# One row of the last weight's second part in four transfers of 25, 25, 64 and 14 partitions

## The chip, the cores and the metric

The kernel runs on one core of a Trainium2 chip. The metric is the device time of one execution in microseconds (us). Engines are named as the profile names them: PE (TensorE's matmuls), PEld (its weight loads), DVE (VectorE), ACT (ScalarE), POOL (GpSimd) and SP (SyncE); a q behind a name means its queue of instructions. Sixteen DMA engines serve the core and move all data between HBM and the on-chip memory.

## The reference

One token passes a transformer block. It is attention over a long cache, and then a gated feed-forward network; the batch is 1 and the query length is 1.

```python
h  = x + attention(layernorm(x), k_cache, v_cache, wq, wo)
# x [1,1,1024]; k_cache, v_cache [1,4,65536,128]; wq [1024,4096]; wo [4096,1024]
# attention: 32 heads of 128, 8 heads to each of 4 cache groups, softmax(q k / sqrt(128)) v
h2 = h + (gelu(layernorm(h) @ w_gate) * (layernorm(h) @ w_up)) @ w_down
# w_gate, w_up [1024,3584]; w_down [3584,1024]; all bfloat16
```

## The kernel before, in words

All weights and both caches are read from HBM once, in all 173 MB, into one buffer `ring` of four slots (`slot`, L183), 32 KB per partition each. All these transfers are issued on SP's queue, in the order of the code. Operations are recorded by `Flow.op` and `Flow.dma` (L31, L69) and issued by `Flow.issue` (L76) with the waits that follow from the keys they read and write, so most instructions carry line 95 in the profile.

The stages are: the layer norm and the query projection (wq, two transfers); eight attention steps, each with two transfers of K and one of V; the output projection (wo); the second layer norm; gate (w_gate, 7 MB), up (w_up, 7 MB) and down (w_down, 7 MB). Within the steps PE runs a loop (`pe_loop`, L415) that takes tokens from the other engines.

The change is in the down projection. Its 3,584 rows are laid on 128 partitions in two blocks. `wa` (L577) holds FA = 16 rows per partition, in slot 0, and is one transfer. `wb` (L578) holds the other FB = 12 rows per partition, in slot 1, and comes in three transfers (L582): FB - FZ = 8 rows, FZ - 1 = 3 rows and 1 row per partition. A row is 1,024 bfloat16 numbers, 2 KB. So a transfer of the eight rows moves 16 KB into each partition. In HBM a partition's twelve rows are one run of 24 KB (`wb_src`, L579).

Each of the four transfers has a landing semaphore: `r_sem[0]`, `r_sem[1]`, `k_sem[0]` and `k_sem[1]`. A transfer raises its semaphore by 16 in all when it has landed. `Flow.dma` gives back the count that the semaphore then has, and `parts` keeps it with the rows (L585).

`wa` is issued when gate's last matmul has read slot 0 (key R0). The others are behind it on SP's queue; their slot 1 (key R1) is free by then as well, and no other wait is between them.

After all recorded work PE runs the down projection (L600 to L605): for each part, four matmuls that keep it busy ahead of the first two parts (`stay_busy`, L596), a wait for the part's semaphore, and then eight matmuls of one row each (`down`, L590), 128 x 32 by 128 x 128, for each of the part's rows. In all these are 28 x 8 = 224 matmuls. They add into two banks that already hold h. Two casts, on DVE (L607) and ACT (L608), then write the result `h2`, and SP stores it (L609).

Of the kernel before, what the change touches and what calls it, by code (L numbers as in the profile page):

```python
# [108 lines left out]
def kernel(  # L109
# [14 lines left out]
    P = 128  # L124
# [58 lines left out]
    def slot(i, n=1):  # L183
        return ring[:, i * CW:(i + n) * CW]

    f = Flow(nc, tc)
# [312 lines left out]
    FA = CW // D  # L499
# [78 lines left out]
    wb = slot(1)[:, 0:FB * D].rearrange("p (e n) -> p e n", e=FB)  # L578
    wb_src = B_w_down[P * FA:F, :].rearrange("(p e) n -> p e n", p=P)  # L579
    parts = [(wa, 0, FA, f.dma("sp", wa, B_w_down[0:P * FA, :].rearrange("(p e) n -> p e n", p=P), after=["R0"], inc=(r_sem[0], 16)), r_sem[0])]  # L580
    e0 = 0
    for i, z in enumerate((FB - FZ, FZ - 1, 1)):  # L582
        part = wb[:, e0:e0 + z, :]
        s = (r_sem[1], k_sem[0], k_sem[1])[i]
        parts.append((part, FA + e0, z, f.dma("sp", part, wb_src[:, e0:e0 + z, :], after=["R1"] if i == 0 else [], inc=(s, 16)), s))  # L585
        e0 += z
    with tc.tile_critical(no_gpsimd_drain=True):
        f.issue()
# [51 lines left out]
```

## Time and profile before

| what | value |
|---|---|
| time, median of 3 runs | 409.96 us (409.71 to 410.44) |
| the profiled execution: its time, its span | 409.71 us, 407.8 us |
| busy: PE, PEld, DVE, ACT, POOL | 234.8, 105.8, 202.5, 39.5, 19.2 us |
| read from HBM | 173.02 MB, 424 GB/s over the span |
| w_down's four transfers issued by SP | from 377.01 us, 2.24 us in all |
| from issue to landing, w_down's 4096, 2048, 768 and 256 KB | 20.4, 25.0, 25.9 and 26.0 us |
| last weight load of the down projection | 404.85 us |
| the two casts | start at 405.34 us |
| the store of the result issued | 405.71 us |

The span reaches from the first to the last instruction of the program. The page divides it into 40 equal slices; a digit is the busy share of a slice in tenths, and the DMA row is the mean over the sixteen DMA engines. Beside instructions, the trace records each DMA packet (start, duration, bytes and queue, not the number of its engine) and each single increment of a landing semaphore. Times within the execution are from the start of the span.

### The profile page before, as it was taken

To read this page: it belongs to the slowest core of one execution; us is meant where nothing else is said; L and a number is where in the kernel's file an instruction comes from. 1 tells how busy PE (TensorE), PEld (TensorE's weight loads), DVE (VectorE), ACT (ScalarE), POOL (GpSimd) and SP (SyncE) were. 2 spreads that over 40 slices of the span, in tenths; PEclk is the share of its full clock that TensorE was granted. 3 is DMA by queue.
4 is the path that set the end of the run, shared out by engine and by line. 5 is a ranking of instruction groups with operands and counts; after the bars stand their busy time and mean duration, and the time that the engine had idled before them with its cause. 6 is when DMAs were issued, how large, how long until landed. Compare 5 with 4: busy or idle time off the path is not lost. (4 is left out here: it accounts for less than half of the span.)

```text
span 407.8 us, 3909 instructions
## 1 busy us (share of the span) xinstructions
PE 234.8 (58%) x1645; PEld 105.8 (26%) x1647; DVE 202.5 (50%) x174; ACT 39.5 (10%) x141; POOL 19.2 (5%) x39
## 2 busy tenths in 40 slices
PE   0433855585577368734973686557465747365376
PEld 0211322232232133212321232223132223142324
DVE  1218860876089328924781687089508941010210
ACT  1000003000300300030003000300220021000000
POOL 4210000001000000010000001000000000012000
PEclk9955995599569967978796689689976976565668
DMA  8999999999999999999998999999999999999995
GB/s 344 427 421 452 415 460 411 460 418 412 453 460 418 411 425 488 418 408 421 476 437 376 453 424 444 421 460 418 411 453 466 418 418 424 452 440 435 399 413 220
DMA packets 4815, 173.12 MB, mean 424 GB/s; under 512 B 580, under 2 KB 584, under 8 KB 840
## 3 DMA queue, kind: packets, MB, share of 16 engines
q1 hardware_dynamic: 4760, 173.02, 98.5%
q8 instruction: 5, 0.08, 0.1%
q14 instruction: 2, 0.02, 0.0%
q10 hardware_dynamic: 48, 0.00, 0.0%
HBM read 173.02 MB, written 0.00 MB: 424 GB/s over the span
## 5 line engine op out<-in xcount | busy, mean ns | idle before, releaser
L95 DVE STREAM_TRANSPOSE ktb<-ring 128x4096 f32<-128x4096 f32 x32 | 141.1, 4418 | 83.4 <-DMA ring<-in_A_k_cache_dram 83.4
L427 PE MATMUL bank<-ktb,qs 128*128 128x512 bf16 x512 | 132.6, 418 | 61.3 <-PEq L413 61.3
L427 PEld LDWEIGHTS bank<-ktb,qs 128*128 128x128 bf16 x512 | 51.5, 104 | 139.2 <-issue 93.6
L439 PE MATMUL bank<-ring,pt 128*32 128x512 bf16 x512 | 46.3, 541 | 36.5 <-PEq L413 36.5
L95 ACT ACTIVATE pt<-sc,nb 128x256 bf16<-128x256 f32 x64 | 31.5, 494 | 255.3 <-DVE nb L95 255.3
L439 PEld LDWEIGHTS bank<-ring,pt 128*32 128x32 bf16 x512 | 19.4, 131 | 60.2 <-issue 57.3
L95 DVE STREAM_TRANSPOSE sc<-bank 128x512 f32<-128x512 f32 x32 | 22.2, 695 | 24.6 <-PE bank L427 24.6
L95 PE MATMUL bank<-ring,xz 128*32 128x512 bf16 (+1 forms) x192 | 19.2, 587 | 17.2 <-DMA ring<-in_B_w_gate_dram 5.2
L95 DVE TENSOR_REDUCE mx<-sc 128x8 f32<-128x1536 f32 (+1 forms) x16 | 19.5, 1219 | 0.5
L95 DVE STREAM_TRANSPOSE ktb<-bank 128x512 f32<-128x512 f32 (+1 forms) x6 | 4.0, 672 | 31.3 <-PE bank L95 30.9
L95 POOL COPY qs<-qsel 32x128 bf16<-32x128 bf16 x16 | 7.8, 490 | 231.4 <-PE bank L427 216.8
L95 PEld LDWEIGHTS bank<-ring,xz 128*32 128x32 bf16 x192 | 7.5, 141 | 26.9 <-issue 15.9
L95 ACT ACTIVATION_READ_ACCUMULATOR pt<-sc,nb 128x1 f32 x64 | 12.0, 187 | 0.0
L448 PE MATMUL bank<-sel,acc_sb 128*128 128x8 f32 x64 | 8.2, 255 | 6.2 <-PEq L413 6.2
L431 PE MATMUL bank<-ident_f,mx 128*8 128x128 f32 x8 | 2.2, 269 | 14.6 <-PEq L413 14.6
L448 PEld LDWEIGHTS bank<-sel,acc_sb 128*128 128x128 f32 x64 | 7.7, 191 | 10.0 <-issue 10.0
L95 PE MATMUL bank<-ring,ktb 128*32 128x512 bf16 x64 | 6.4, 586 | 5.9 <-DMA ring<-in_A_wo_dram 5.9
L95 ACT COPY acc_sb<-bank 128x512 f32<-128x512 f32 x8 | 4.7, 586 | 48.9 <-PE bank L439 48.9
L95 DVE TENSOR_TENSOR h_col<-bank,x_col 128x8 f32<-128x8 f32 x1 | 0.2, 167 | 14.8 <-PE bank L95 14.8
L95 PE MATMUL bank<-sel,ktb 128*128 128x16 f32 (+1 forms) x24 | 5.2, 356 | 3.5 <-DVE bank L95 2.7
L95 POOL MEMSET ktb<- 128x1024 bf16 (+2 forms) x3 | 3.5, 1164 | 75.8 <-PE bank L427 75.8
L433 PE MATMUL bank<-diag,ones_f 8*128 8x8 f32 x16 | 3.7, 299 | 5.7 <-PEq L413 5.7
(85 smaller groups left out, 60.9 us busy)
## 6 DMA issues: line engine op xcount, KB each, us to landing
ring<-in_A_k_cache_dram SPq DMA_DIRECT2D x16, 4096.0 KB, 24.9
ring<-in_A_wq_dram SPq DMA_DIRECT2D x2, 4096.0 KB, 16.7
ring<-in_B_w_gate_dram SPq DMA_DIRECT2D x1, 7168.0 KB, 26.9
ring<-in_B_w_up_dram SPq DMA_DIRECT2D x1, 7168.0 KB, 27.2
ring<-in_B_w_down_dram SPq DMA_DIRECT2D x1, 4096.0 KB, 20.4
ring<-in_B_w_down_dram SPq DMA_DIRECT2D x1, 2048.0 KB, 25.0
ring<-in_B_w_down_dram SPq DMA_DIRECT2D x1, 768.0 KB, 25.9
ring<-in_B_w_down_dram SPq DMA_DIRECT2D x1, 256.0 KB, 26.0
```

Source lines behind the costliest of these rows:

```text
L95: ins = getattr(self.eng[e], o["call"])(**o["kw"])
L427: m = nc.tensor.matmul(bank[c][:], lhsT=qs[:, jt].rearrange("p s c -> p (s c)")[:, s * P:(s + 1) * P], rhs=mv[:, :, J, :, u], start=(s == ...
L431: nc.tensor.transpose(out=mxT_ps, in_=mx1[:], identity=ident_f[:]).then_inc(s_step, 1)
L433: nc.tensor.matmul(bc_ps, lhsT=ones_f[0:rep, :], rhs=diag[:], start=True, stop=True).then_inc(s_step, 1)
L439: m = nc.tensor.matmul(acc[32 * q:32 * q + 32, :], lhsT=pt[:, c, n, :, :].rearrange("p h s -> p (h s)"), rhs=v_sb[:, c, :, n, :], start=(c ...
L448: m = nc.tensor.matmul(o_ps, lhsT=acc_sb[:, u * Dh:(u + 1) * Dh], rhs=sel[:, u:SQ:NS], start=(u == 0), stop=(u == NS - 1))
```

## The change

The eight-row transfer of `wb` becomes five transfers. Row 0 of every partition goes first, in four: partitions 0 to 24, 25 to 49, 50 to 113 and 114 to 127. Rows 1 to 7 of all partitions follow in one. All five raise the same semaphore, `r_sem[1]`, by 16 each, and PE's wait for the part is for the count after the fifth. The three-row and the one-row transfer are as before, behind them on the queue. No matmul changes, nor the order of rows in which they run.

```diff
     for i, z in enumerate((FB - FZ, FZ - 1, 1)):
         part = wb[:, e0:e0 + z, :]
         s = (r_sem[1], k_sem[0], k_sem[1])[i]
-        parts.append((part, FA + e0, z, f.dma("sp", part, wb_src[:, e0:e0 + z, :], after=["R1"] if i == 0 else [], inc=(s, 16)), s))
+        if i == 0:
+            for p0, p1 in ((0, 25), (25, 50), (50, 114), (114, P)):
+                f.dma("sp", wb[p0:p1, 0, :], wb_src[p0:p1, 0, :], after=["R1"], inc=(s, 16))
+            at = f.dma("sp", part[:, 1:, :], wb_src[:, 1:z, :], after=["R1"], inc=(s, 16))
+        else:
+            at = f.dma("sp", part, wb_src[:, e0:e0 + z, :], inc=(s, 16))
+        parts.append((part, FA + e0, z, at, s))
         e0 += z
```

## The prediction

> **What bounds the kernel now.** I began with the profile's page: the DMA row by slice, the queues, then the chain that ended last.
>
> ```profile
> DMA  8999999999999999999998999999999999999995
> ...
> q1 hardware_dynamic: 4760, 173.02, 98.5%
> ...
> DVE h L607 0%
> ```
>
> The DMA engines are busy in every slice but the first and the last ones, and SP's queue alone fills 98.5% of sixteen engines' span. The chain stops at the last cast (L607), so what comes before that cast has to be read from the timeline of PE at the end and from PE's waits from 370 us on:
>
> ```profile
> 397.48 3.40 PE L593 MATMUL bank<-ring,ktb 128*32 128x128 bf16 x128
> 401.05 0.81 PE L598 MATMUL bank<-qs 128*128 128x512 bf16 x3 [0.16 <-issue]
> 402.38 0.62 PE L593 MATMUL bank<-ring,ktb 128*32 128x128 bf16 x30 [0.53 <-DMA ring<-in_B_w_down_dram]
> 403.50 1.65 PE L593 MATMUL bank<-ring,ktb 128*32 128x128 bf16 x66 [0.49 <-issue]
> ```
>
> ```profile
> PE bank L95 <- DMA ring<-in_B_w_gate_dram: 5.2, 1, 5.2
> PE bank L95 <- DMA ring<-in_B_w_up_dram: 5.0, 1, 5.0
> ```
>
> PE waits for the transfers of gate, of up, and again before the rows of w_down: the kernel is a stream of 173 MB, and its end is the last rows' landing plus a tail. The busy times by stage show that tail:
>
> ```profile
> 397.40:402.40 5.00, 4.31 (x136) 3.56 (x137) 0.00 (x0) 0.00 (x0) 0.00 (x0) 0.69 0.98 407
> 402.40:404.90 2.50, 1.85 (x92) 1.33 (x96) 0.00 (x0) 0.00 (x0) 0.00 (x0) 1.00 0.32 124
> 404.90:407.80 2.90, 0.25 (x8) 0.07 (x8) 0.28 (x1) 0.26 (x1) 0.00 (x0) 0.92 0.00 1
> ```
>
> The last two columns are DMA share and GB/s. From 402.4 to 404.9 the share is 0.32: most engines are done and a few work on. The trace's sixteen increments of each landing semaphore say how few. For the last row of w_down ten come at 402.97 to 403.47 and six at 403.76, 404.29, 404.51, 404.65, 404.67 and 404.81. Five of the six were as far behind in the sixteen-row transfer (eleven by 396.08, the last at 397.44). Packets of kind "instruction" (8 or 16 KB, at 33.2, 99.8, 143.2, 358.0, 376.9 and 401.1 us) each went before one more late increment. As packets follow one another on an engine without a gap (the next starts 4 ns before the last one's end), an engine never makes it up. The trace does not number the engines.
>
> **The change, part by part.** Bytes and matmuls stay. Row zero of the eight-row part (2 KB in each of 128 partitions) goes in transfers of 25, 25, 64 and 14 partitions, and the other seven rows in one.
>
> *Who carries them.* In the transfers of the trace, engines that take part carry equal shares: 128 partitions are eight packets on each of sixteen engines, x_in's 32 are two on each, and the output's four partitions are one packet on each of four (its semaphore rises once at 406.17 and four times from 406.86 to 406.90). In equal shares 25 goes on five engines (or one), 64 on sixteen, 14 on fourteen. [...] Rows leave open whether it is one five twice or two fives; I take the same five, since nothing in the code tells one transfer's engines from the other's.
>
> *What each engine then does.* Pace of a 16 KB packet 607 ns (611 less the 4 of overlap), of a 2 KB packet 80, of the 4-byte semaphore packet about 6. Between them lie (607 - 80) / 14,336 B = 0.0368 ns a byte, so 14 KB cost 607 - 75 = 532. Before, every engine has 8 x 607 + 6 = 4,862 ns for this part. After:
> - five engines carry 5 + 5 + 4 + 1 = 15 rows and five semaphore packets: 8 x 532 + 15 x 80 + 30 = 5,486, so +0.62 us;
> - nine carry 4 + 1 rows: 4,256 + 400 + 18 = 4,674, so -0.19 us;
> - two carry 4 rows: 4,256 + 320 + 12 = 4,588, so -0.27 us.
>
> With two different fives, ten engines have 10 rows: +0.22 us.
>
> *Which of them sets the end.* Every part waits for all sixteen engines. An early engine (403.47 at most) plus 0.62 ends at 404.09, inside the 404.81 of now: free. One of the five that land from 404.29 on, plus 0.62, lands at 404.91 to 405.43: the end moves by +0.10 to +0.62. If five of sixteen engines are drawn blindly, none of these late five is among them with 462 / 4,368 = 0.11; with one or more, the mean over which is the latest is +0.47 us.
>
> *Rows written by other engines.* [...] Below: no cost, as the last 2 KB rows still take 84 ns beside 6 KB packets of other engines. Above: every one of 15 rows at twice its 80 ns, +1.2 us. A gain is excluded, since an engine alone already runs at 16,384 / 607 = 27.0 B/ns without gaps. I take a little under the middle, +0.5 us: the five engines write 25 neighbouring partitions at once, but the rows are then half over. [...]
>
> *Issue.* Four more on SP's queue. The four of w_down took 2.24 us together, single ones 0.33 to 0.88 us, so 1.3 to 3.5 us more, over by 383 us at the latest. The part's first packet starts at 395.1 and SP's next work is the output at 405.71: hidden by 12 us. Parts two and three are issued behind them, and have until 400. Without that cover it would cost those 1.3 to 3.5 us.
>
> *PE.* Its wait asks for all five transfers, and queued behind it are the last 96 matmuls and both casts. 66 matmuls in 1.65 us are 25 ns each, so 96 need 2.4 us, and 0.49 us idle (ended by "issue") lie among them: from 402.38 that is about 405.2, as late as the last landing's chain (404.81 and eight matmuls). So a late part one is not given back, unless PE's 0.49 us gap stands at a fixed time and covers part of it.
>
> **Sum.** +0.47 (late engines) + 0.5 (shared places) + 0 (issue) = about +0.95 us. The profiled execution took 409.71 us (span 407.8, 1.9 around it), 0.25 under the median of 409.96; it would be 410.66, and the median 410.9.
>
> **Rivals.** A difference of 0.2%, 0.82 us, is about what a measurement of this kernel can tell from no change.
> 1. *The forecast: late engines get more, and rows collide* (0.42): +0.8 to +1.8 us, the upper end 0.62 + 1.2; 410.8 to 411.8.
> 2. *Late engines get more, nothing collides* (0.26): +0.10 to +0.62 us, 410.1 to 410.6, within 0.2%. For it: 2 KB packets at a constant 84 ns. [...]
> 3. *The five are early, and the change levels* (0.18): the late ones have three or four rows less, so the end comes 0.19 to 0.27 us sooner: 409.7 to 409.8, not slower. It decides where none of the late five is among the five. For it: 0.62 us fits in the early engines' 1.3 us of room. Against: 0.11 by lot; I go above it because the instruction packets hit six different engines, one after another, which is not a blind draw and may run past the five.
> 4. *Faster by over 0.2%* (0.08): the mean of the sixteen last increments is 403.66, so perfect levelling is worth 1.15 us (408.8). It would need some ten rows off each late engine, and the change takes at most four; only an unseen effect on PE's 0.49 us gap could add.
> 5. *25 partitions go on one engine* (0.06): it has 55 rows, 4,256 + 4,400 + 30 = 8,686 ns, +3.8 us; early now it ends near 407.0 (+2.2), late at +3.8: 412.2 to 413.8. Equal shares allow it; the output's four engines for four partitions speak against it.
>
> **How the numbers follow.** Slower: 0.42 + 0.06 = 0.48. Within 0.2%: 0.26 + 0.18 = 0.44. Faster: 0.08. The range holds cases 1 to 3, with 0.2 us for the spread of medians at the low end: 409.4 to 411.8; cases 4 and 5, 0.14 together, lie outside. The likeliest case's own range is 410.8 to 411.8.
>
> **What would show it.** Right: in the profile after, the part has 128 packets of 2 KB, and some of them last over 84 ns; the part's semaphore has its last increment past 402.9 instead of 402.34, and the cast at L607 starts near 406.3. The two 25s would raise the semaphore by eleven counts at once, then five. Wrong: all those packets at 84 ns (no collision; case 2 or 3); the last increments of part one at 402.15 with the early ones at 401.5 (case 3); one engine with some fifty 2 KB packets in a row (case 5). If the six late increments are gone or are others in the profile after, the lateness is no property of the program, and the step on which engines are late fails.

## The result and the profile after

The changed kernel takes 411.23 us (median of 8 runs, 411.04 to 411.59), the kernel before 409.88 us in the same series: +1.35 us, a ratio of 1.0033 (95% interval 1.0022 to 1.0044). So it is slower, and by more than 0.2%. The profiled execution took 411.21 us with a span of 409.2.

The page's lines that answer to those of before hardly differ: the stream is as full, and the chain again stops at a cast, now L613.

```profile
DMA  8999999999999999999999998999899999999995
...
q1 hardware_dynamic: 4928, 173.02, 98.5%
...
DVE h L613 0%
```

The timeline of PE shows where the time goes (start, duration, line, operation; in brackets the idle time before and what ended it):

```profile
398.38 3.60 PE L599 MATMUL bank<-ring,ktb 128*32 128x128 bf16 x128 [0.69 <-DMA ring<-in_B_w_down_dram]
402.32 0.99 PE L604 MATMUL bank<-qs 128*128 128x512 bf16 x3 [0.33 <-issue]
403.68 1.26 PE L599 MATMUL bank<-ring,ktb 128*32 128x128 bf16 x64 [0.37 <-DMA ring<-in_B_w_down_dram]
405.54 0.93 PE L599 MATMUL bank<-ring,ktb 128*32 128x128 bf16 x32 [0.59 <-DMA ring<-in_B_w_down_dram]
```

PE waits for w_down three times. Its second part starts at 403.68 instead of 402.38, after a last increment at 403.64. The first part is later too, by 0.9 us, though the change does not touch its transfer: its last increment is at 398.34 instead of 397.44. The last row's increments run from 403.94 to 406.13 (402.97 to 404.81 before), and the casts start at 406.71, 1.37 us later.

The busy times by stage show the loss at its place. First before, then after; the last two columns are DMA share and GB/s.

```profile
395.30:399.20 3.90, 2.62 (x71) 2.03 (x76) 0.15 (x1) 0.00 (x0) 0.00 (x0) 0.73 0.97 412
```

```profile
395.30:399.20 3.90, 2.31 (x35) 1.25 (x40) 0.00 (x0) 0.00 (x0) 0.00 (x0) 0.57 1.02 298
399.20:402.40 3.20, 2.87 (x109) 2.73 (x99) 0.00 (x0) 0.00 (x0) 0.00 (x0) 0.50 0.99 412
```

The engines are just as busy and move 298 GB/s instead of 412; from 399.2 on the rate is back. (A packet counts in the stretch in which it starts, so a share can come out over 1.) 114 GB/s over 3.9 us are 0.44 MB, which at 412 GB/s is 1.08 us. The packets say the same: of the part's 2 KB packets 100 take over 90 ns, up to 182 (84 in the last row before); the first 14 KB packets take up to 967 ns (540 afterwards); and four 32 KB packets of the first part, on engines that were late, took 1,844 to 1,874 ns instead of 1,218. All sixteen engines are slowed, those too that still work on an untouched transfer: at 396.5 us sixteen packets are in flight, and every one takes longer than packets of its size take earlier or later (2 KB 141 to 153 ns, 14 KB 779 to 967, 32 KB 1,844 to 1,874); in the kernel before none does (16 KB 611 to 619, 32 KB 1,221). The mean of the last row's sixteen increments went from 403.66 to 404.87, by 1.21 us. So 1.21 of the 1.32 us by which the last increment moved is lost by the sixteen engines on the mean, and 0.11 is a wider spread.

### The profile page after: what moved, and what is told of

It reads as the page before. It is cut to its first block, busy times and chain, and to the rows that moved or that the text cites. A ratio compares the mean times of both kernels' runs of the same rounds, so it can differ in the third digit from the quotient of the medians.

```text
span 409.2 us, 3913 instructions
## 1 busy us (share of the span) xinstructions
PE 231.3 (57%) x1645; PEld 104.2 (25%) x1647; DVE 202.7 (50%) x174; ACT 39.4 (10%) x141; POOL 19.2 (5%) x39
## 5 line engine op out<-in xcount | busy, mean ns | idle before, releaser
L427 PE MATMUL bank<-ktb,qs 128*128 128x512 bf16 x512 | 131.1, 415 | 62.9 <-PEq L413 62.9
L95 PE MATMUL bank<-ring,xz 128*32 128x512 bf16 (+1 forms) x192 | 18.2, 559 | 18.2 <-DMA ring<-in_B_w_gate_dram 6.2
L599 PE MATMUL bank<-ring,ktb 128*32 128x128 bf16 x224 | 5.7, 272 | 1.8 <-DMA ring<-in_B_w_down_dram 1.7
```

The lines of the kernel that those rows point to most:

```text
L95: ins = getattr(self.eng[e], o["call"])(**o["kw"])
L427: m = nc.tensor.matmul(bank[c][:], lhsT=qs[:, jt].rearrange("p s c -> p (s c)")[:, s * P:(s + 1) * P], rhs=mv[:, :, J, :, u], start=(s == ...
L599: nc.tensor.matmul((d_ps, d_odd)[q // 2][32 * q:32 * q + 32, :], lhsT=a_row[:, AZ - m:AZ - m + 32], rhs=w_row[:, j * OB:(j + 1) * OB], sta ...
```

## Experiments

Theory A: rows written into partitions that several engines then share crowd one another and slow all engines. Theory B: the unequal shares make late engines later. Theory C: small packets ahead of large ones are slow by themselves.

**Row 0 in one transfer of 128 partitions.**

```diff
-            for p0, p1 in ((0, 25), (25, 50), (50, 114), (114, P)):
-                f.dma("sp", wb[p0:p1, 0, :], wb_src[p0:p1, 0, :], after=["R1"], inc=(s, 16))
+            f.dma("sp", wb[:, 0, :], wb_src[:, 0, :], after=["R1"], inc=(s, 16))
```

> [...] Theory A (rows written by other engines than usual crowd each other, and that slows all sixteen): no cost, 2 KB packets at 84 ns, time within 0.1 us of before (8 x 532 + 8 x 80 + 12 = 4,908 ns an engine against 4,862). Theory B (unequal shares make the late engines later): the same, within 0.1 us of before. Theory C (2 KB packets ahead of 14 KB ones are slow wherever they go, because of how they read HBM): as the changed kernel, +1.2 us, 2 KB packets at 100 to 180 ns.

Measured: 409.95 us against 409.85, ratio 1.0001 (0.9992 to 1.0010). The same two sizes of packet as in the change, 2 and 14 KB, and no loss of rate:

```profile
395.30:399.20 3.90, 2.58 (x80) 1.85 (x84) 0.00 (x0) 0.00 (x0) 0.00 (x0) 0.84 1.01 420
```

The 2 KB packets average 84.5 ns; two of row 0's 128 took over 90. C falls: neither the size nor the order of the packets costs anything that the medians show. The profiled execution also tells how much two profiles can differ with equal medians: its casts start at 405.65, 0.31 later than before's.

**Row 0 in four equal quarters.**

```diff
-            for p0, p1 in ((0, 25), (25, 50), (50, 114), (114, P)):
+            for p0, p1 in ((0, 32), (32, 64), (64, 96), (96, P)):
```

> [...] Theory A: slow, +0.8 to +1.6 us over before, 2 KB packets well over 84 ns, and the mean of the sixteen last increments of the last row later by about as much as the end is. Theory B: within 0.1 us of before, since no engine has more than another. Theory C: +1.2 us.

Measured: 411.30 us, +1.45, ratio 1.0033 (1.0021 to 1.0045), the same as the change. The mean of the last increments moved by 1.48 us to 405.15.

```profile
395.30:399.20 3.90, 1.86 (x28) 0.91 (x32) 0.07 (x1) 0.00 (x0) 0.00 (x0) 0.71 1.02 278
```

With equal shares B expects nothing, and yet the whole loss is there. The numbers 25, 25, 64 and 14 are not needed for it.

**The change for two rows.**

```diff
-            for p0, p1 in ((0, 25), (25, 50), (50, 114), (114, P)):
-                f.dma("sp", wb[p0:p1, 0, :], wb_src[p0:p1, 0, :], after=["R1"], inc=(s, 16))
-            at = f.dma("sp", part[:, 1:, :], wb_src[:, 1:z, :], after=["R1"], inc=(s, 16))
+            for e in (0, 1):
+                for p0, p1 in ((0, 25), (25, 50), (50, 114), (114, P)):
+                    f.dma("sp", wb[p0:p1, e, :], wb_src[p0:p1, e, :], after=["R1"], inc=(s, 16))
+            at = f.dma("sp", part[:, 2:, :], wb_src[:, 2:z, :], after=["R1"], inc=(s, 16))
```

> The change twice: rows 0 and 1 each go in four transfers of 25, 25, 64 and 14 partitions, the other six rows in one. Theory A: the crowded stretch is twice as long, +2.4 to +2.9 us over before (twice the changed kernel's +1.35), the mean of the last increments later by about 2.4 us. Theory B: the five engines get 1.25 us more, and the end moves by at most that over before, or 0.62 over the changed kernel. Theory C: as A, +2.4 us.

Measured: 413.08 us, +3.23, ratio 1.0077 (1.0063 to 1.0091), somewhat over A's 2.4 to 2.9. The mean of the last increments moved by 2.75 us, the last one by 3.28. B's bound of 1.25 is out. The dose counts. Part of what goes beyond twice is not of this part: in the profiled execution the increments at the landing of up were already 0.52 us later in the mean than before's (0.37 the last one), so that 2.23 us of the mean, less than A's 2.4, came behind it.

**Which engines are late.** Fifteen marks behind the last transfer:

```diff
+    for k in range(1, 16):
+        s = tc.alloc_semaphore("mark_%d" % k)
+        marks.append(s)
+        f.dma("sp", spare_k[k][0:k], wb_src[0:k, 0, 0:32], inc=(s, 16))
...
+        for s in marks:
+            nc.sync.wait_ge(s, 16)
```

> The kernel before, and behind its last transfer fifteen tiny ones of k = 1 to 15 partitions with 64 bytes each, every one with a landing semaphore of its own. If k partitions go on the k lowest engines, the increments of mark k are those of engines 0 to k-1, and what mark k has more than mark k-1 is engine k-1: that gives each engine's finish by number, and so which engines are late. Theory B as the prediction used it expects at least one of the five latest among engines 0 to 4 (by lot 0.89), and that the change moves the end by 0.10 to 0.62 us through it. Theory A needs none there. Time: within 0.5 us of before, as the store waits for the marks.

After the jump that each semaphore makes at issue, mark 1 rose at 403.32. Mark 2 rose at 403.50 and 403.93, so the first is engine 0 again, some 0.18 us later, and the second is engine 1. In this way down to mark 15, less 0.17 to 0.20 us for each mark that an engine has carried, every engine's last-row increment gets a number (the order in which the engines join the marks):

```
engine      0       1       2       3       4       5       6       9       14      the other seven
us        403.14  403.76  403.39  404.30  403.18  404.88  404.54  404.62  404.87  402.96 to 403.35
```

So of the five latest only engine 3 is among 0 to 4, and it is the earliest of them, 0.58 us ahead of the last. With 0.62 us more it ends at 404.92: the shares alone would move the end by 0.04 us. The time was 412.55 us, one run, 2.7 over before and not within 0.5: the store waited for the marks, the last of which rose at 406.89. The numbering holds for this execution; the kernel before has the same pattern of increments (403.76, 404.29 and four later ones).

**Unequal shares with nothing crowded.** Seven rows more for engines 0 to 4:

```diff
+    f.dma("sp", spare[0:17:4], wb_src[0:17:4, 1:8, :], after=["R1"], inc=(s_spare, 16))
...
+        nc.sync.wait_ge(s_spare, 16)
```

> The kernel before with one transfer more ahead of the eight-row part: rows 1 to 7 of partitions 0, 4, 8, 12 and 16 a second time, into a spare tile, 14 KB on each of engines 0 to 4 (70 KB that nobody reads; the store waits for them). Unequal shares alone, in partitions that lie four apart. Theory B as the prediction had it: the five engines get 532 + 6 ns, and the end moves by up to 0.54 us, by the prediction's mean 0.4. With the marks' numbering (engine 3 the latest of the five, at 404.3, 0.58 ahead of the last one): +0.0 to +0.1 us, mean of the last increments +0.17 (5 x 0.54 / 16). Theory A expects no slow packets, if four apart is where these engines write anyway.

Measured: 410.44 us, +0.56, ratio 1.0015 (1.0006 to 1.0024). Most of it is the wait that was added for the spare rows. The casts start at 405.46, 0.12 later than before, but the store is issued 0.63 us after the cast's end instead of 0.09, though the spare rows had landed at 397.54:

```profile
405.46 0.28 DVE L612 CAST h<-bank 64x128 bf16<-64x128 f32 x1 [10.43 <-PEq L603]
406.37 0.29 SPq L614 DMA_DIRECT2D out_dram<-h  x1
```

The five packets took 542 ns, and no other packet was slower than usual; from 395.3 to 399.2 the engines moved 413 GB/s (412 before). Shares alone are worth +0.12 us on the casts, less than the 0.31 by which two profiles differed above. The mean of the increments is +0.43 instead of +0.17, but at the landing of up it was already 0.27 us later than before's; the rest, 0.16, is what the shares should give.

**The same bytes on the same engines, next to each other** (the edit is against the run with the partitions apart).

```diff
-    f.dma("sp", spare[0:17:4], wb_src[0:17:4, 1:8, :], after=["R1"], inc=(s_spare, 16))
+    f.dma("sp", spare[0:5], wb_src[0:5, 1:8, :], after=["R1"], inc=(s_spare, 16))
```

> The same extra 70 KB on the same five engines, but in partitions 0 to 4, next to each other. Theory B: exactly as with the partitions apart. Theory A (what counts is that several engines write into the same few neighbouring partitions): slower than with the partitions apart by 0.3 to 1.6 us, 14 KB packets well over 540 ns (four at one place would take 4 x 532 = 2.1 us), and the mean of the last increments later by more than 0.17 us. If only the engines that write there are slowed, the other engines' packets stay at their usual 611 and 1,218 ns; if the slowing spreads, theirs are longer too.

Measured: 411.59 us, 1.15 over the run with the partitions apart; the casts start at 406.71, 1.25 later than there. Only the partitions differ, and with them the rows' places in HBM, 24 KB from one to the next instead of 96 KB; this pair alone does not tell the two apart.

```profile
395.30:399.20 3.90, 3.17 (x64) 1.72 (x68) 0.00 (x0) 0.00 (x0) 0.00 (x0) 0.56 0.95 335
```

The five packets average 710 ns (up to 981), and the slowing spreads: 16 KB packets of the part behind take up to 1,527 ns instead of 619, and 32 KB ones of the part ahead up to 1,635 instead of 1,221. At 396.0 us sixteen packets are in flight, none of them one of the five, and all sixteen are slow; with the partitions apart none is. Seventy KB cost over a microsecond.

**The part in two halves.**

```diff
-            for p0, p1 in ((0, 25), (25, 50), (50, 114), (114, P)):
-                f.dma("sp", wb[p0:p1, 0, :], wb_src[p0:p1, 0, :], after=["R1"], inc=(s, 16))
-            at = f.dma("sp", part[:, 1:, :], wb_src[:, 1:z, :], after=["R1"], inc=(s, 16))
+            for p0, p1 in ((0, 64), (64, P)):
+                at = f.dma("sp", wb[p0:p1, 0:z, :], wb_src[p0:p1, 0:z, :], after=["R1"], inc=(s, 16))
```

> The eight-row part as two transfers of 16 KB packets, partitions 0 to 63 and 64 to 127: equal shares, no small packet, one transfer more. Theory A: if 64 neighbouring partitions take data at only half of the rate of 128, the 2 MB need 4.9 us more, so +2 to +5 us, 16 KB packets near 1,200 ns. Theory B and C: within 0.2 us of before.

Measured: 417.15 us, +7.27, ratio 1.0185 (1.0169 to 1.0200), above A's own range.

```profile
395.30:399.20 3.90, 1.89 (x4) 0.43 (x4) 0.00 (x0) 0.00 (x0) 0.00 (x0) 0.50 1.04 164
399.20:402.40 3.20, 1.83 (x72) 1.83 (x76) 0.00 (x0) 0.00 (x0) 0.00 (x0) 0.50 0.97 215
```

Equal shares, large packets and two transfers: rate of 164 to 215 GB/s, and 16 KB packets at 1,312 ns on the mean. That is about half of the 412 GB/s or less, and the first part's packets suffer beside (32 KB in up to 3,315 ns).

**The four transfers for the last row instead** (the edit is against the kernel before).

```diff
-        parts.append((part, FA + e0, z, f.dma("sp", part, wb_src[:, e0:e0 + z, :], after=["R1"] if i == 0 else [], inc=(s, 16)), s))
+        if i == 0:
+            at = f.dma("sp", part, wb_src[:, e0:e0 + z, :], after=["R1"], inc=(s, 16))
+        elif i == 1:
+            at = f.dma("sp", part, wb_src[:, e0:e0 + z, :], inc=(s, 16))
+        else:
+            for p0, p1 in ((0, 25), (25, 50), (50, 114), (114, P)):
+                at = f.dma("sp", wb[p0:p1, e0, :], wb_src[p0:p1, e0, :], inc=(s, 16))
+        parts.append((part, FA + e0, z, at, s))
```

> The eight-row part whole again, and the four transfers of 25, 25, 64 and 14 partitions for the last part's one row instead, where ten engines have 1.3 us of room. Theory A: the crowding takes about as many engine-microseconds as in the changed kernel, but the early engines lose it in time that they would be idle: +0.2 to +0.8 us over before, less than the change's +1.35. Theory B with the marks' numbering: engine 3, 404.30 + 7 x 0.08 = 404.86, so +0.05 us; with the prediction's mean +0.47. Were levelling worth anything, this would show a gain of up to 0.3 us.

Measured: 410.48 us, +0.60, ratio 1.0015 (1.0006 to 1.0024). The last increment comes at 405.36 (404.81 before). The same transfers cost less than half of the change where ten engines have room, but the end gains nothing from levelling.

**Which partitions.** Rows 1 to 7 of 64 partitions a second time, once for 32 to 95 and once for 0 to 63:

```diff
+    f.dma("sp", spare[32:96], wb_src[32:96, 1:8, :], after=["R1"], inc=(s_spare, 16))
...
+        nc.sync.wait_ge(s_spare, 16)
```

The second run has `0:64` in place of `32:96`.

> The kernel before with one transfer more ahead of the eight-row part: rows 1 to 7 of partitions 32 to 95 a second time, into a spare tile, 14 KB packets, four on each of sixteen engines, 896 KB that nobody reads (the store waits for them, which by the runs with 70 KB costs about 0.5 us by itself). [...] If any transfer of fewer than 128 partitions is slow: +4 to +6 us, packets near 1,100 ns.

> The same with partitions 0 to 63. [...] If any transfer of fewer than 128 partitions is slow, or none is: as the run with the middle 64.

Measured: 412.72 us with the middle 64 (+2.81, ratio 1.0065, 1.0048 to 1.0082), 417.13 with the lower 64 (+7.22, 1.0180, 1.0158 to 1.0201). The first line is of the middle, the second of the lower 64:

```profile
395.30:399.20 3.90, 3.37 (x68) 1.99 (x72) 0.00 (x0) 0.00 (x0) 0.00 (x0) 0.56 1.00 423
```

```profile
395.30:399.20 3.90, 1.89 (x4) 0.43 (x4) 0.00 (x0) 0.00 (x0) 0.00 (x0) 0.50 1.05 180
```

Number of transfers, engines, packet size and bytes are the same, and so is the pattern of the rows in HBM, 24 KB from one to the next. The middle 64 go at the full rate (423 GB/s, 541 ns a packet), the lower 64 at 180 GB/s (1,219 ns). So it is neither that a transfer has fewer than 128 partitions, nor the number of bytes, but which partitions lie together: a packet into the lower 64 takes 1,219 / 541 = 2.25 times as long as one into the middle 64. Why these partitions are slow together and those are not, the runs do not show.

One rival is not separated: that an engine is slow by itself in partitions that another engine writes in the transfers of 128. The trace does not give an engine's partitions, so no run tests it. Packets of untouched transfers were slow as well (32 KB in up to 3,124 ns with the lower 64), which it alone does not explain.

## Why the prediction was right, and which of its terms were not

The forecast case came true: slower, 411.23 us in the range of 409.4 to 411.8 and in the case's own 410.8 to 411.8, with +1.35 us where the sum gave +0.95. But its two terms were not the sizes that it gave them: the late engines' was some 0.4 us too large, the shared places' some 0.7 too small. That the sum came so near is partly luck.

- *What bounds the kernel.* Right: the last landing set the end before and after (last increment +1.32 us, casts +1.37).
- *Who carries the rows.* Right. The part's semaphore has three rises at issue, at 377.23, 377.59 and 378.83, then 56 single increments: 5 + 5 + 16 + 14 + 16. The marks add that each mark's engines are those of the mark before and one more, which no row of before shows. The last row's increments fit both 25s on the same five. An estimate from the marks' times and the prediction's shares (+0.62 for engines 0 to 4, -0.19 for the next nine, -0.27 for the last two), all moved by 1.11 us, meets each of the sixteen within 0.13 us, with engine 3 as the last; with the second 25 on engines 5 to 9 it misses by up to 0.35.
- *Late engines, +0.47.* Mis-sized: 0.04 by the marks, 0.12 by the run with shares alone. The step that failed is the mean over a blind draw. Engine 3 was late but had 0.58 us of slack to the last, which the 0.62 us just used up. That the lateness belongs to the program held: at the landing of up five increments are as late in the profile after (386.59 to 387.65) as before (386.66 to 387.72).
- *Rows written by other engines, +0.5.* Mis-sized: 1.1 to 1.2, the height of the upper bound but not by its way. The term was my estimate: no run shows which partitions an engine writes, so none shows rows written by other engines than usual. What the runs show in its place is that row 0 costs nothing in one transfer of 128 partitions (2 KB packets at 84.5 ns) and 1.45 us in four quarters. The bound charged fifteen rows on five engines; the runs show all sixteen engines slowed. The row that I leaned on for a low cost (2 KB packets at 84 ns beside other engines' 6 KB) was of one transfer of 128 partitions, so it said nothing of a row in pieces. The other reason, that rows are half over, missed that the slowing reaches packets of other transfers (32 KB in up to 1,874 ns).
- *Issue, hidden.* Right. The eight issues took 3.66 us instead of 2.24, and ended at 380.0.
- *PE.* The 0.49 us gap is gone in the profile after, and PE waits 0.59 us before the last 32 matmuls: the late part one cost nothing of its own, since the last landing was later still.
- *The signs.* The part's last increment at 403.64 (past 402.9) and packets over 84 ns came as named; the cast at 406.71, not 406.3, by the larger second term.

Rival 2 fell with the 182 ns packets, rival 3 with engine 3 and with the run on the last row, rival 5 with the 56 increments. Rival 4 lacked room: one of the five latest engines got more rows, not fewer, and crowding took more than levelling could give.

## What to carry to other kernels

Before a full-width transfer is cut by partitions, look at which partitions fall into one piece: 32 to 95 went at 423 GB/s, 0 to 63 at 180, and 70 KB into five neighbouring partitions cost over 1 us across all engines. Cut along the rows within each partition instead (the free dimension), where the same packets cost nothing measurable (1.0001). And when a stream is full on every engine, compare the mean and the spread of the sixteen landing increments: here the moved mean was lost rate (1.21 of the 1.32 us, at 298 GB/s instead of 412), and the wider spread was the small rest (0.11). Look at an earlier landing of the same execution first: it can already be late, by 0.52 us in the run with two rows.

## What was not expected of the hardware

The slowing is not confined to the transfers that were cut or added. In the changed kernel packets of an untouched transfer went from 1,218 to 1,874 ns, and with five packets of 14 KB next to each other 16 KB packets of another transfer took up to 1,527 ns, and all sixteen engines were slow at once. How it spreads from one engine to the next was not measured. After each of the six 8 or 16 KB instruction packets from 33.2 to 401.1 us one more increment was late in every landing that followed, six by the end. That such a packet ran on the engine that was late is inferred from the order alone.
